# A retention layer and a Mish feed-forward layer: the second product of eight blocks as seven quarter products

## The chip, the cores and the metric

The kernel runs on one core of one Trainium2 chip. Its engines run side by side, each through its own queue in order: TensorE (PE, with its weight loads shown apart as PEld), VectorE (DVE), ScalarE (ACT), GpSimd (POOL) and SyncE (SP), which here issues most of the transfers. The metric is the device time of one launch in microseconds (us).

## What is computed

First a retention layer, a recurrence over 768 steps for 4 batches and 8 heads of width 64; its output, 3072 tokens by 512, goes through two matrix products with Mish between them.

```python
for t in range(S):
    state = gamma[None, :, None, None] * state + np.einsum('bhd,bhe->bhde', k[:, :, t], v[:, :, t])
    y[:, :, t] = scale * np.einsum('bhd,bhde->bhe', q[:, :, t], state)
...
h = x @ w_in                                         # 3072x512 by 512x2048
sp = np.where(h > 20.0, h, np.log1p(np.exp(np.minimum(h, 20.0))))
g = h * np.tanh(sp)
return (g @ w_out).astype(np.float32)                # 3072x2048 by 2048x512
```

## The kernel before

**Chunks and blocks.** The sequence is cut into 24 chunks of 128 tokens, 6 for each batch. The feed-forward part works on 11 blocks: block 0 has 4 chunks, blocks 1 to 10 have two each (256 tokens). Blocks are counted from 0 throughout. Inputs, weights and intermediate values are in fp16 where PE reads them; sums are in fp32 in PSUM.

**A block's two products.** `g1` (line 395) makes one group of the first product, 8 matmuls of 256 columns into one PSUM bank (`h_ps`), and one ACT activation (Mish) from it into a `g` tile that holds two of the 16 slices of 128 rows of the hidden width. Eight groups make the block's first product. The second product takes each of the block's two chunks by itself: 16 matmuls of 512 columns (`g2_mm`, line 410) with a slice of `g` as the stationary operand and a slice of `w_out` as the moving one, summed in one bank (`o_ps`), which DVE copies to SBUF (`g2_out`, line 416). SP stores it. The last chunk of the last block is made in two halves of 256 columns.

**The retention steps** for the next block are put between these matmuls by hand. `casts` (line 209) scales q, k and v into fp16 on POOL. `turn_by_dma` (225) turns q and k by a transfer. `scores_two` (362) makes q times k on PE, and DVE multiplies them by a mask. `outer_two` (369) makes the state's increments on PE; `state` (289) adds and scales them on DVE with L293, or with L296 and L297. `y_two` (379) makes the layer's output from scores and state, and ACT copies it to `xt`, which the next block's first product reads. `next_chunk(g)` (518) casts ahead, turns chunk g and loads chunk g + 2.

**What sets the order.** The kernel is written in the order in which each engine's queue then runs; nothing is rescheduled. The main loop goes through 16 steps u for each block, 8 for the first product and 8 for the second. `plan_of` (524) lists what follows which step: for blocks after the first, casts and `next_chunk` after steps 1, 4, 8 and 12, scores after 7, outer after 10 and y after 13. Stores wait in a list until their step. Tiles come from pools in rotation: the tag `mm` has four PSUM banks for `h_ps` and `o_ps`, the tag `at` two pairs of banks for scores, increments and y. A tile's writer waits until the one that had the buffer before has been read. POOL runs as far ahead as loads and buffers allow, whatever step its casts are written in.

Of the kernel before, what the change touches and what calls it, by code (L numbers as in the profile page):

```python
# [16 lines left out]
def kernel(  # L17
# [150 lines left out]
    def store_due(now):  # L168
        while stores and stores[0][0] <= now:
            _, dst, osb = stores.pop(0)  # L170
            nc.sync.dma_start(dst, osb)
# [223 lines left out]
    def g1(blk, u):  # L395
        nt = BLOCKS[blk] * C
        per = TB // nt
        h_ps = mmps.tile([P, per, nt], FP32, name="h_ps", tag="mm")
        for j in range(per):
            s, f = divmod(u * per + j, FPS)  # L400
            for bp in range(NBP):
                nc.tensor.matmul(  # L402
                    h_ps[:, j], wins[s][f // 2][:, bp, f % 2 * P:(f % 2 + 1) * P], xts[blk][:, bp, :nt],
                    start=(bp == 0), stop=(bp == NBP - 1))
# [1 line left out]
        nc.scalar.activation(gt, h_ps, AF.Mish, scale=inv_boost3)  # L406
# [9 lines left out]
    def g2_out(o_ps, blk, t, due, cols=slice(None)):  # L416
        osb = op.tile(list(o_ps.shape), FP32, name="osb", tag="osb")
        nc.vector.tensor_copy(osb, o_ps)  # L418
# [102 lines left out]

    def plan_of(blk):
        a = first[blk] + 4
        early = blk == 1
        plan = {1: [(cast_to, a + 1)],
                (1 if early else 4): [(cast_to, a + 1), (next_chunk, a)],
                (5 if early else 8): [(cast_to, a + 2)],
                (5 if early else 12): [(cast_to, a + 2), (next_chunk, a + 1)]}  # L530
        if blk + 1 < len(BLOCKS):
            plan[10 if early else 7] = [(scores_two, blk + 1)]
            plan[12 if early else 10] = [(outer_two, blk + 1)]
            plan[14 if early else 13] = [(y_two, blk + 1)]
        return plan

    first_block()
    for blk in range(1, len(BLOCKS)):
# [4 lines left out]
        for u in range(nu):
            store_due(u)
            if u < n1:
                g1(blk, u)
            else:
                t, part = divmod(u - n1, 4)
                if last and t == BLOCKS[blk] - 1:
                    if part % 2 == 0:  # L550
                        half = slice(part // 2 * (d_model // 2), (part // 2 + 1) * (d_model // 2))
                        o_ps = mmps.tile([P, d_model // 2], FP32, name="o_ps", tag="mm")
                        for fb in range(NFB):
                            g2_mm(o_ps, blk, t, fb, half)
                        g2_out(o_ps, blk, t, 0, half)
                        store_due(nu)
                    continue
# [39 lines left out]
```

## Time and profile before

| | |
|---|---|
| median of 3 runs | 214.64 us (214.62 to 214.94) |
| profiled execution, its own time | 214.51 us |
| span of its trace | 212.7 us |
| granted PE clock | 1.000 |
| first matmul of blocks 2, 3, 4, 5 | 67.58, 83.69, 99.59, 115.48 us |
| first matmul of blocks 6, 7, 8, 9, 10 | 131.60, 147.49, 163.39, 179.51, 195.41 us |
| POOL's last cast | 162.79 us |

The profiled execution is 1.8 us longer than the span from its first to its last instruction. Rows of a group give the line, engine, operation, the tile that is written and those that are read, shapes, a count, busy time and the mean of one in ns, and then the idle time ahead of it with what ended it. Rows of a timeline start with the start in us and the length; rows of the same kind are merged, with their count. "Busy" of pipelined matmuls counts overlaps, so a matmul's cost is read from the starts of what stands before and behind it.

### The profile page before, as it was taken

How to read it: one execution, taken by the hardware profiler on the slowest of the kernel's cores; microseconds unless marked ns; L12 is line 12 of the kernel's file. 1: busy time of each engine (PE TensorE's matmuls, PEld its weight loads, DVE VectorE, ACT ScalarE, POOL GpSimd, SP SyncE). 2: the span in 40 equal slices, each digit the busy share in tenths (PEclk: the TensorE clock that was granted, in tenths of full speed). 3: DMA queues.
4: the chain of work that ended last, by engine and by line, in shares of the span. 5: the costliest groups of instructions: out<-in, count | busy, mean ns of one | idle time of the engine just before them, and what ended most of it. 6: DMA issues, size and time to landing. Idle time of an engine off the chain costs nothing.

```text
span 212.7 us, 4169 instructions
## 1 busy us (share of the span) xinstructions
PE 206.9 (97%) x1733; PEld 133.5 (63%) x1733; DVE 84.6 (40%) x113; ACT 77.9 (37%) x122; POOL 75.2 (35%) x72
## 2 busy tenths in 40 slices
PE   7999999999999999999999999999999999999993
PEld 2564444456856856856856856856856856856863
DVE  3697444366046065062064065062065065062011
ACT  2443663153612612612612612612612612612610
POOL 2131000509773662666576067066067000000000
PEclk9999999999999999999999999999999999999999
DMA  5999999998999999999993994994893901101102
GB/s 188 230 231 351 385 386 318 264 256 175 194 235 274 184 241 187 251 217 182 248 220 89 215 182 99 208 178 110 203 196 97 151 0 52 49 2 52 49 0 99
DMA packets 99842, 38.56 MB, mean 181 GB/s; under 512 B 90480, under 2 KB 93808, under 8 KB 99824
## 3 DMA queue, kind: packets, MB, share of 16 engines
q1 hardware_dynamic: 96560, 37.50, 78.7%
q10 hardware_dynamic: 3264, 0.81, 2.3%
q8 instruction: 13, 0.21, 0.4%
q14 instruction: 5, 0.04, 0.1%
HBM read 27.29 MB, written 6.29 MB: 158 GB/s over the span
## 4 chain that ended last, share of the span: by engine, by line
PE 81%; DMA 8%; SPq 6%; ACT 1%; DVE 1%; issue 0%; ACTq 0%
PE h_ps L402 36%; PE o_ps L412 36%; DMA wi<-in_moe_w_in_dram 5%; SPq L120 5%; DMA kf<-in_k_dram 3%; PE y_ps L313 3%; PE at L263 3%; PE y_ps L303 2%; PE u_ps L281 2%; SPq L138 1%; ACT xt L390 1%; SPq L179 0%; DVE win L155 0%; ACT qk L218 0%; PE t_ps L251 0%
## 5 line engine op out<-in xcount | busy, mean ns | idle before, releaser
L412 PE MATMUL o_ps<-wout,g 128*128 128x512 f16 (+1 forms) x400 | 89.2, 371 | 0.0
L402 PE MATMUL h_ps<-xt,win 128*128 128x256 f16 (+1 forms) x704 | 85.7, 282 | 0.6 <-ACT xt L390 0.2
L402 PEld LDWEIGHTS <-win 128*128 128x128 f16 x704 | 68.7, 98 | 18.3 <-DVE win L155 1.1
L406 ACT ACTIVATE g<-h_ps 128x512 f16<-128x512 f32 x96 | 57.3, 597 | 41.2 <-PE h_ps L402 40.6
L412 PEld LDWEIGHTS <-g 128*128 128x128 f16 x400 | 36.9, 98 | 38.0 <-issue 0.3
L273 DVE TENSOR_TENSOR am<-at,tri 128x1024 f16<-128x1024 f32 x20 | 23.6, 1219 | 63.7 <-PE at L263 63.7
L215 POOL TENSOR_TENSOR qk<-qf,qvs 128x512 f16<-128x512 f32 x20 | 20.9, 1045 | 66.2 <-DMA qf<-in_q_dram 58.6
L390 ACT CAST xt<-y_ps 128x1024 f16<-128x1024 f32 x10 | 10.1, 1012 | 62.9 <-PE y_ps L313 62.9
L221 POOL TENSOR_TENSOR v<-vf,qvs 128x512 f16<-128x512 f32 x24 | 25.0, 1042 | 18.0 <-DMA vf<-in_v_dram 16.7
L418 DVE COPY osb<-o_ps 128x512 f32<-128x512 f32 (+1 forms) x25 | 16.5, 666 | 33.4 <-PE o_ps L412 33.4
L220 POOL TENSOR_SCALAR qk<-kf 128x512 f16<-128x512 f32 x18 | 27.8, 1542 | 3.8 <-DMA kf<-in_k_dram 2.5
L241 PE MATMUL at<-ident 128*128 128x512 f16 (+1 forms) x34 | 10.9, 449 | 1.3 <-POOL ident L81 1.3
L296 DVE TENSOR_TENSOR su<-u_ps,st 128x512 f32<-128x512 f32 x13 | 9.0, 692 | 6.4 <-PE u_ps L281 6.2
L297 DVE TENSOR_TENSOR st<-su,gcm 128x512 f16<-128x512 f32 x13 | 10.6, 818 | 0.4
L313 PE MATMUL y_ps<-am,v 128*64 128x128 f16 x192 | 8.2, 223 | 0.2 <-DVE am L273 0.2
L218 ACT ACTIVATE qk<-kf 128x512 f16<-128x512 f32 x6 | 3.8, 630 | 12.1 <-DMA kf<-in_k_dram 12.1
L155 DVE CAST win<-wi 128x1024 f16<-128x1024 f32 x8 | 5.4, 692 | 5.6 <-DMA wi<-in_moe_w_in_dram 5.6
L281 PEld LDWEIGHTS <-qk 128*128 128x128 f16 x80 | 5.3, 98 | 2.7
L303 PEld LDWEIGHTS <-st 128*128 128x128 f16 x80 | 5.3, 98 | 2.7
L313 PEld LDWEIGHTS <-v 128*64 128x64 f16 x192 | 5.8, 109 | 1.7 <-issue 0.3
L281 PE MATMUL u_ps<-v,qk 128*128 128x128 f16 x80 | 6.8, 220 | 0.0
L241 PEld LDWEIGHTS <-ident 128*128 128x128 f16 x34 | 3.5, 114 | 5.1 <-issue 3.3
(42 smaller groups left out, 59.1 us busy)
## 6 DMA issues: line engine op xcount, KB each, us to landing
kf<-in_k_dram SPq DMA_DIRECT2D x23, 256.0 KB, 4.9
vf<-in_v_dram SPq DMA_DIRECT2D x23, 256.0 KB, 5.1
out_dram<-osb SPq DMA_DIRECT2D x23, 256.0 KB, 2.5
qf<-in_q_dram SPq DMA_DIRECT2D x19, 256.0 KB, 4.1
wt<-in_moe_w_out_dram SPq DMA_DIRECT2D x3, 1024.0 KB, 10.1
wi<-in_moe_w_in_dram SPq DMA_DIRECT2D x4, 512.0 KB, 7.3
wi<-in_moe_w_in_dram SPq DMA_DIRECT2D x2, 1024.0 KB, 11.6
qfirst<-in_q_dram SPq DMA_DIRECT2D x2, 512.0 KB, 4.6
```

Source lines behind the costliest of these rows:

```text
L215: nc.gpsimd.tensor_tensor(q16, qf, qs.unsqueeze(2).broadcast_to((P, H, D)), op=ALU.mult)
L220: nc.gpsimd.tensor_scalar(k16, kf, BOOST, None, op0=ALU.mult)
L221: nc.gpsimd.tensor_tensor(v16, vf, vs.unsqueeze(2).broadcast_to((P, H, D)), op=ALU.mult)
L241: nc.tensor.matmul(ats[g][:, 0, :m], ident, ident.unsqueeze(1).broadcast_to((P, m, P)), start=True, stop=True)
L273: nc.vector.tensor_tensor(am[:, :, i:i + n], at[:, :, i:i + n], keep.unsqueeze(1).unsqueeze(1).broadcast_to((P, 2, n, C)), op=ALU.mult)
L281: nc.tensor.matmul(u_ps[:, i], k16[:, 2 * i:2 * i + 2], v16[:, 2 * i:2 * i + 2], start=onto is None or i == 0, stop=onto is None, skip_gro ...
L313: nc.tensor.matmul(y(i)[o:o + 64], v16[:, 2 * i + hh], am[:, hh, i], start=fresh(i), stop=True, skip_group_check=True)
L390: nc.scalar.copy(xt[:, :, :2 * C], y_ps.rearrange("p i j c -> p i (j c)"))
L402: nc.tensor.matmul(h_ps[:, j], wins[s][f // 2][:, bp, f % 2 * P:(f % 2 + 1) * P], xts[blk][:, bp, :nt], start=(bp == 0), stop=(bp == NBP - 1))
L406: nc.scalar.activation(gt, h_ps, AF.Mish, scale=inv_boost3)
L412: nc.tensor.matmul(o_ps, gts[blk, fb][:, t * P:(t + 1) * P], wouts[s][:, f, cols], start=(fb == 0), stop=(fb == NFB - 1))
L418: nc.vector.tensor_copy(osb, o_ps)
```

## The change

From block 3 on, the second product of a block is one product of a 256 x 2048 matrix A (the two chunks of `g`) with the 2048 x 512 matrix B (`w_out`), each cut into quarters. Seven products of quarters (each 8 matmuls of 256 columns) and their sums take the place of the eight that the plain form needs:

- sums of A: S1 = A21 + A22, S2 = S1 - A11, S3 = A11 - A21, S4 = A12 - S2
- sums of B, made once in block 2: T1 = B12 - B11, T2 = B22 - T1, T3 = B22 - B12, T4 = B21 - T2
- C11 = A11 B11 + A12 B21; U2 = A11 B11 + S2 T2; U3 = U2 + S3 T3; C22 = U3 + S1 T1; C12 = U2 + S1 T1 + S4 B22; C21 = U3 + A22 T4

DVE makes the sums in fp16: in each of these blocks 16 operations of 128 x 256 elements, of which the 8 for S1 and S2 (`sums_a`) stand behind groups 4 to 7 of the first product. PSUM sums are kept across products; ACT copies (`snap`) an intermediate value out where it is used twice. DVE adds or copies the four quarters of C into the block's two store tiles. The sums of B take the weights' staging buffers, eight DVE operations of 128 x 1024, one after each of block 2's steps 0 to 7.

The retention steps are moved for these blocks: outer stands after step 0, scores after step 3, y inside the second product between the products S2 T2 and S1 T1. `next_chunk` stands after steps 1 and 7; the stores of a block stand in steps 1 and 2 of the next. Block 2 has `next_chunk` after steps 2 and 8. The last block stores its four quarters one by one.

```diff
+    def weight_sums(half):
+        n, hf = NFB // 2, d_model // 2
...
+        return [
+            lambda: nc.vector.tensor_tensor(t1, b12, b11, op=sub),
+            lambda: nc.vector.tensor_tensor(t2, b22, t1, op=sub),
+            lambda: nc.vector.tensor_tensor(t3, b22, b12, op=sub),
+            lambda: nc.vector.tensor_tensor(t4, b21, t2, op=sub),
+        ]
...
+    def sums_a(blk, u):
+        (s1, s2, _, _), a11, _, a21, a22 = sum_views(blk, u)
+        nc.vector.tensor_tensor(s1, a21, a22, op=ALU.add)
+        nc.vector.tensor_tensor(s2, s1, a11, op=ALU.subtract)
+
+    def sums_b(blk):
+        for u in range(NFB // 4):
+            (_, _, s3, _), a11, _, a21, _ = sum_views(blk, u)
+            nc.vector.tensor_tensor(s3, a11, a21, op=ALU.subtract)
+
+    def sums_c(blk):
+        for u in range(NFB // 4):
+            (_, s2, _, s4), _, a12, _, _ = sum_views(blk, u)
+            nc.vector.tensor_tensor(s4, a12, s2, op=ALU.subtract)
+
+    def seven(blk, hooks, last):
+        n, hf = NFB // 2, d_model // 2
+        ps = [mmps.tile([P, hf], FP32, name="o_ps", tag="mm") for _ in range(3)]
+        pb, pe, px = ps
...
+        def snap(o_ps):
+            x = op.tile([P, hf], FP32, name="snap", tag="snap", bufs=3)
+            nc.scalar.copy(x, o_ps)
+            return x
+
+        def done(i, j, o_ps, plus=None):
+            dst = osb[i][:, j * hf:(j + 1) * hf]
+            if plus is None:
+                nc.vector.tensor_copy(dst, o_ps)
+            else:
+                nc.vector.tensor_tensor(dst, o_ps, plus, op=ALU.add)
...
+        mm(px, a(0, 0), b(0, 0), True)
+        m1 = snap(px)
+        mm(pb, a(0, 1), b(1, 0), True)
+        sums_b(blk)
+        done(0, 0, pb, m1)
+        mm(px, s(2), t(2))
+        u2 = snap(px)
+        sums_c(blk)
+        for fn, *args in hooks:
+            fn(*args)
+        mm(pe, s(1), t(1), True)
+        m5 = snap(pe)
+        mm(px, s(3), t(3))
+        done(1, 1, px, m5)
+        mm(pe, s(4), b(1, 1))
+        done(0, 1, pe, u2)
+        mm(px, a(1, 1), t(4))
+        done(1, 0, px)
+        if not last:
+            for i in range(2):
+                row0 = (first[blk] + i) * P
+                stores.append((1 + i, out[row0:row0 + P], osb[i]))
...
     def plan_of(blk):
         a = first[blk] + 4
-        early = blk == 1
+        if blk >= SEVEN:
+            plan = {1: [(cast_to, a + 1), (next_chunk, a)],
+                    7: [(cast_to, a + 2), (next_chunk, a + 1)]}
+            if blk + 1 < len(BLOCKS):
+                plan[0] = [(outer_two, blk + 1)]
+                plan[3] = [(scores_two, blk + 1)]
+            return plan
...
+        extra = weight_sums(0) + weight_sums(1) if blk + 1 == SEVEN else []
+        for u in range(n1 if blk >= SEVEN else 2 * n1):
             store_due(u)
             if u < n1:
                 g1(blk, u)
+                if blk >= SEVEN and u >= n1 // 2:
+                    sums_a(blk, u - n1 // 2)
...
+            if extra:
+                extra.pop(0)()
+        if blk >= SEVEN:
+            seven(blk, [] if last else [(y_two, blk + 1)], last)
+    store_due(2 * NFB)
```

How DVE's queue changes. Before, these rows are one block's work on DVE, in the order of the queue: the two copies of the second product, the two masks, and the state of two chunks.

```order
L418 COPY osb<-o_ps 128x512 x2
L273 TENSOR_TENSOR am<-at,tri 128x1024 x2
L296 TENSOR_TENSOR su<-u_ps,st 128x512
L297 TENSOR_TENSOR st<-su,gcm 128x512
L296 TENSOR_TENSOR su<-u_ps,st 128x512
```

In the changed kernel, at the end of a block's first product and in its second: the last pair of S1 and S2, S3's four parts, the add that ends C11, S4's four parts, and the add that ends C22. `g_1466` to `g_1529` are the tiles of groups 0 to 3, `g_1562` to `g_1601` those of groups 4 to 7.

```order
L463 TENSOR_TENSOR gsum<-g_1529,g_1601 128x256 [waits Activation_49]
L464 TENSOR_TENSOR gsum<-gsum,g_1529 128x256 [waits DVE_49]
L469 TENSOR_TENSOR gsum<-g_1466 128x256
L469 TENSOR_TENSOR gsum<-g_1493 128x256
L469 TENSOR_TENSOR gsum<-g_1518 128x256
L469 TENSOR_TENSOR gsum<-g_1529 128x256
L510 TENSOR_TENSOR osb<-o_ps,snap 128x256 [waits DMAHW3_49,PE_49,Activation_49]
L474 TENSOR_TENSOR gsum<-g_1562,gsum 128x256
L474 TENSOR_TENSOR gsum<-g_1575,gsum 128x256
L474 TENSOR_TENSOR gsum<-g_1588,gsum 128x256
L474 TENSOR_TENSOR gsum<-g_1601,gsum 128x256 [waits DVE_49]
L510 TENSOR_TENSOR osb<-o_ps,snap 128x256 [waits DMAHW0_49,PE_49,Activation_49]
```

The sums and adds stand in one queue, so the adds for C wait behind all sums that are written ahead of them.

On PE, where the product A12 B21 ends and S2 T2 begins:

```order
L496 MATMUL o_ps<-wout_595,g_1601 128x256
L496 LDWEIGHTS gsum [waits DVE_49]
L496 MATMUL o_ps<-tmat,gsum 128x256 [waits Activation_49]
L496 LDWEIGHTS gsum
L496 MATMUL o_ps<-tmat,gsum 128x256
L496 LDWEIGHTS gsum [waits DVE_49]
```

Every second weight load of this product waits for a part of S2 from DVE, and its first matmul for ACT's copy of the bank that it adds to. Before, the second product waited for activations alone.

On SP, the transfers of one block and the start of the next, before:

```order
L171 DMA out_dram<-osb 128x512 x2
L227 DMA_TRANSPOSE qkt<-qk_1633 128x8x128
L120 DMA qf<-in_q_dram 128x8x64
L120 DMA kf<-in_k_dram 128x8x64
L120 DMA vf<-in_v_dram 128x8x64
L227 DMA_TRANSPOSE qkt<-qk_1740 128x8x128
```

and in the changed kernel:

```order
L173 DMA out_dram<-osb 128x512
L229 DMA_TRANSPOSE qkt<-qk_1760 128x8x128
L122 DMA qf<-in_q_dram 128x8x64
L122 DMA kf<-in_k_dram 128x8x64
L122 DMA vf<-in_v_dram 128x8x64
L173 DMA out_dram<-osb 128x512
L229 DMA_TRANSPOSE qkt<-qk_1870 128x8x128
```

The two stores, which stood together ahead of a pair of chunks, now stand one ahead of each chunk; the first holds the transposes and loads of its block until the block ahead has its C11 and C12.

More of the change, by code (lines that the diff above doesn't have):

```diff
@@ L106 @@
     xts, gts, wins, wouts, wtmps = {}, {}, {}, {}, {}
+    gtiles, tmats, gsums = {}, [], []
+    SEVEN = 3
     nload, ncast = [0], [0]
@@ L424, in g2_out @@
         stores.append((due, dst, osb))
+    def weight_sums(half):
+        n, hf = NFB // 2, d_model // 2
+        if half == 0:
+            tmats.extend(
+                wstage.tile([P, 2, n, hf], FP16, name="tmat", tag="wt", bufs=4)
+                for _ in range(2))
+            gsums.extend(
+                wstage.tile([P, 4, n, P], FP16, name="gsum", tag="wt", bufs=4)
+                for _ in range(2))
+        f = slice(half * FPS, (half + 1) * FPS)
+        t1, t2 = tmats[0][:, 0, f], tmats[0][:, 1, f]
+        t3, t4 = tmats[1][:, 0, f], tmats[1][:, 1, f]
+        b11, b12 = wouts[half][:, :, :hf], wouts[half][:, :, hf:]
+        b21, b22 = wouts[half + 2][:, :, :hf], wouts[half + 2][:, :, hf:]
+        sub = ALU.subtract
+        return [
[4 more added lines that the diff above has]
+        ]
@@ new lines, in sum_views @@
+    def sum_views(blk, u):
+        s = gsums[blk % 2]
+        f = slice(2 * u, 2 * u + 2)
+        lo, hi = gtiles[blk, u], gtiles[blk, u + NFB // 4]
+        return ([s[:, i, f] for i in range(4)],
+                lo[:, :, :P], hi[:, :, :P], lo[:, :, P:], hi[:, :, P:])
+    def sums_a(blk, u):
[6 more added lines that the diff above has]
+            nc.vector.tensor_tensor(s3, a11, a21, op=ALU.subtract)
@@ new lines, in sums_c, with a, b, s @@
+    def sums_c(blk):
[6 more added lines that the diff above has]
+        pb, pe, px = ps
+        osb = [op.tile([P, d_model], FP32, name="osb", tag="osb") for _ in range(2)]
+        def a(i, j):
+            return lambda f: gts[blk, j * n + f][:, i * P:(i + 1) * P]
+        def b(i, j):
+            return lambda f: wouts[(i * n + f) // FPS][:, f % FPS, j * hf:(j + 1) * hf]
+        def s(i):
+            return lambda f: gsums[blk % 2][:, i - 1, f]
+        def t(i):
+            return lambda f: tmats[(i - 1) // 2][:, (i - 1) % 2, f]
+        def mm(o_ps, x, w, first=False):
+            for f in range(n):
+                nc.tensor.matmul(
+                    o_ps, x(f), w(f), start=first and f == 0, stop=f == n - 1,
+                    skip_group_check=True)
+        def snap(o_ps):
[9 more added lines that the diff above has]
+            row0 = (first[blk] + i) * P
+            if last:
+                nc.sync.dma_start(out[row0:row0 + P, j * hf:(j + 1) * hf], dst)
+        mm(px, a(0, 0), b(0, 0), True)
[18 more added lines that the diff above has]
+            for i in range(2):
+                row0 = (first[blk] + i) * P
+                stores.append((1 + i, out[row0:row0 + P], osb[i]))
@@ L525, in plan_of @@
         a = first[blk] + 4
-        early = blk == 1
-        plan = {1: [(cast_to, a + 1)],
[L528 to L534, printed above, removed]
+        if blk >= SEVEN:
[5 more added lines that the diff above has]
+            return plan
+        early, then_seven = blk == 1, blk + 1 == SEVEN
+        plan = {1: [(cast_to, a + 1)],
+                (1 if early else 2 if then_seven else 4): [(cast_to, a + 1), (next_chunk, a)],
+                (5 if early else 8): [(cast_to, a + 2), (next_chunk, a + 1)]}
+        plan[10 if early else 7] = [(scores_two, blk + 1)]
+        plan[12 if early else 10] = [(outer_two, blk + 1)]
+        plan[14 if early else 13] = [(y_two, blk + 1)]
         return plan
@@ L546 @@
                 g1(blk, u)
+                if blk >= SEVEN and u >= n1 // 2:
+                    sums_a(blk, u - n1 // 2)
             else:
                 t, part = divmod(u - n1, 4)
[L549 to L557, printed above, removed]
                 if part == 0:
```

4 lines of the change are left out of this document (1 added, 3 removed).

## The prediction

> **What bounds the kernel now.** I read the page's busy times first, then its chain of waits, then the table of stretches (one row for each block), then the PE timeline inside one block, and last the timelines of the engines that a block's second product would newly wait for.
>
> ```profile
> span 212.7 us, 4169 instructions
> ...
> PE 206.9 (97%) x1733; PEld 133.5 (63%) x1733; DVE 84.6 (40%) x113; ACT 77.9 (37%) x122; POOL 75.2 (35%) x72
> ...
> PE 81%; DMA 8%; SPq 6%; ACT 1%; DVE 1%; issue 0%; ACTq 0%
> PE h_ps L402 36%; PE o_ps L412 36%; DMA wi<-in_moe_w_in_dram 5%; SPq L120 5%; DMA kf<-in_k_dram 3%; PE y_ps L313 3%; PE at L263 3%; PE y_ps L303 2%; PE u_ps L281 2%; SPq L138 1%; ACT xt L390 1%; SPq L179 0%; DVE win L155 0%; ACT qk L218 0%; PE t_ps L251 0%
> ```
>
> PE sets the time: the chain is 81% PE, in equal parts on the two products. DVE and POOL are idle more than half of the span, but that is a mean over stages. The stretches from one block's first L402 to the next's show the stage that counts:
>
> ```profile
> 99.59:115.48 15.89, 15.89 (x141) 10.92 (x140) 6.14 (x7) 5.79 (x9) 10.04 (x9) 1.00 0.96 207
> 147.49:163.39 15.90, 15.90 (x141) 10.90 (x140) 6.56 (x7) 5.79 (x9) 7.35 (x7) 1.00 0.75 162
> 163.39:179.51 16.12, 16.12 (x145) 11.12 (x144) 6.41 (x8) 5.79 (x9) 0.45 (x1) 1.00 0.38 70
> ```
>
> These are blocks 4, 7 and 8 (counted from 0); the columns are length, then busy time of PE, PEld, DVE, ACT, POOL, then clock and DMA. PE is busy all through at full clock. Up to block 7, POOL works 7 to 10 us of each 16; from block 8 on it has nothing left to cast. Inside block 5:
>
> ```profile
> 115.48 7.15 PE L402 MATMUL h_ps<-xt,win 128*128 128x256 f16 x64
> 122.57 0.62 PE L263 MATMUL at<-qkt 64*128 64x128 f16 x16
> 123.12 2.77 PE L412 MATMUL o_ps<-wout,g 128*128 128x512 f16 x12
> 125.72 0.61 PE L281 MATMUL u_ps<-v,qk 128*128 128x128 f16 x8
> 126.17 2.75 PE L412 MATMUL o_ps<-wout,g 128*128 128x512 f16 x12
> 128.76 0.61 PE L303 MATMUL y_ps<-qkt,st 128*128 128x128 f16 x8
> ...
> 129.87 1.90 PE L412 MATMUL o_ps<-wout,g 128*128 128x512 f16 x8
> 131.60 7.15 PE L402 MATMUL h_ps<-xt,win 128*128 128x256 f16 x64
> ```
>
> From start to start, a 512-column matmul costs 2.60 / 12 = 0.217 us. Scores cost 0.55, outer 0.45, y 1.11.
>
> **The change, part by part.**
>
> *Matmuls.* The rates need the length of one:
>
> ```profile
> L412 PE MATMUL o_ps<-wout,g 128*128 128x512 f16 x368 | 85.7, 380 | 0.0
> L402 PE MATMUL h_ps<-xt,win 128*128 128x256 f16 x640 | 71.5, 273 | 0.3 <-ACT xt L390 0.2
> ...
> L418 DVE COPY osb<-o_ps 128x512 f32<-128x512 f32 x23 | 15.6, 686 | 31.1 <-PE o_ps L412 31.1
> ...
> L206 DVE COPY kt<-t_ps 128x512 f16<-128x512 f16 x4 | 1.7, 422 | 0.5 <-PE t_ps L204 0.3
> ...
> L418 DVE COPY osb<-o_ps 128x256 f32<-128x256 f32 x2 | 0.8, 424 | 2.4 <-PE o_ps L412 2.4
> ```
>
> At 256 columns the step is (7.15 - 0.273) / 63 = 0.109 us. Thirty-two at 0.217 (6.93) become 56 at 0.109 (6.12): 0.81 less a block. The first product keeps its 64, and the moved scores, outer and y keep their counts.
>
> *The sums, if nothing disturbs them.* I count from a block's first matmul and put a group of the first product at 8 x 0.109 = 0.87. PE then has outer 0.87 to 1.32, scores 4.05 to 4.60 (0.10 is lost ahead of scores now too: 115.48 + 6.99 is 122.47, they start at 122.57), the last group done at 8.09; then the products A11 8.15, A12 9.02, S2 9.90, y 10.77, S1 11.88, S3 12.76, S4 13.63, A22 14.50 to 15.38. The 0.06 at 8.09 is new: the first product's bank is read by the activation of group 6, which in these rows of block 6 ends 0.597 after 137.98, when PE (from 131.60) is just done:
>
> ```profile
> 132.74 0.60 ACT L406 ACTIVATE g<-h_ps 128x512 f16<-128x512 f32 x1 [1.69 <-PE h_ps L402]
> ...
> 137.98 0.60 ACT L406 ACTIVATE g<-h_ps 128x512 f16<-128x512 f32 x1 [0.28 <-PE h_ps L402]
> ```
>
> An activation ends 0.87 after its group, so the pairs for the sums are there at 6.33, 7.21, 8.08 and 8.96. No row shows a two-input 16-bit DVE operation of 256 elements. From above it is bounded by 0.424 (256 in 32 bits). From below: 512 take 0.422 in 16 bits and 0.686 in 32 bits, so half the streaming goes, and 256 take about 0.29. I take 0.29, since 16 bits are what L206 has. The masks end near 6.84; S2 would be ready between 7.5 and 9.65, its product needs its parts from 9.90 to 10.55; S3 by 10.9 for 12.76, S4 by 12.3 for 13.63. The three ACT copies (0.4 each) and the adds leave 0.1 to 0.2 us. So undisturbed nothing is late, and a block costs 15.4 in place of 16.12: 0.7 less. This holds for blocks 8 and 9 (1.4) and, without y, for 10 (0.75): **2.15 less**.
>
> *The sums beside POOL.* This decides. Here a DVE operation with both inputs in SBUF (L297) meets POOL's casts:
>
> ```profile
> 94.36 1.04 POOL L215 TENSOR_TENSOR qk<-qf,qvs 128x512 f16<-128x512 f32 x1 [1.77 <-DMA qf<-in_q_dram]
> 95.48 1.81 POOL L220 TENSOR_SCALAR qk<-kf 128x512 f16<-128x512 f32 x1
> ...
> 154.83 1.04 POOL L215 TENSOR_TENSOR qk<-qf,qvs 128x512 f16<-128x512 f32 x1 [7.02 <-DMA qf<-in_q_dram]
> ...
> 159.78 1.04 POOL L215 TENSOR_TENSOR qk<-qf,qvs 128x512 f16<-128x512 f32 x1 [1.21 <-DMA qf<-in_q_dram]
> ```
>
> ```profile
> L297 DVE TENSOR_TENSOR st<-su,gcm x13: 691/693/1528, 45.6 to 190.9; 128x512 f16<-128x512 f32 x13
> ...
> 95.08 0.87 DVE L297 TENSOR_TENSOR st<-su,gcm 128x512 f16<-128x512 f32 x1
> 95.87 0.68 DVE L418 COPY osb<-o_ps 128x512 f32<-128x512 f32 x1
> ...
> 155.02 2.35 DVE L273 TENSOR_TENSOR am<-at,tri 128x1024 f16<-128x1024 f32 x2 [6.63 <-PE at L263]
> ...
> 159.84 1.53 DVE L297 TENSOR_TENSOR st<-su,gcm 128x512 f16<-128x512 f32 x1
> ```
>
> Its 13 runs take 0.691 at least and 0.693 in the middle; two of the long ones are shown. Both times it ends 0.55 after POOL's cast does (95.40 to 95.95, 160.82 to 161.37), as if it had waited for the whole cast; and POOL's next cast of k, 1.49 in a row below, stretches to 1.81. The masks, with one input in PSUM, run through POOL's 154.83 cast at full speed. All 16 sums of a block have both inputs in SBUF. The Trainium skill states this as a rule (SBUF — State Buffer, "Who interferes with whom"): such a DVE instruction contends with a GpSimd one that reads SBUF, and whichever has the port blocks the other for its whole length. These rows agree; by the rule 16-bit sums are blocked alike, without it the sum would be the first rival's.
>
> When does POOL work? It casts as loads land, and SP issues them behind the transposes and stores:
>
> ```profile
> 87.23 1.28 SPq L171 DMA_DIRECT2D out_dram<-osb  x2
> ...
> 116.86 1.29 SPq L227 DMA_TRANSPOSE qkt<-qk  x1
> 118.21 0.57 SPq L120 DMA_DIRECT2D qf<-in_q_dram  x1
> ...
> 119.51 0.74 SPq L120 DMA_DIRECT2D vf<-in_v_dram  x1
> ...
> 122.84 0.58 SPq L120 DMA_DIRECT2D qf<-in_q_dram  x1
> ```
>
> ```profile
> 122.00 1.04 POOL L215 TENSOR_TENSOR qk<-qf,qvs 128x512 f16<-128x512 f32 x1 [5.83 <-DMA qf<-in_q_dram]
> 123.16 1.49 POOL L220 TENSOR_SCALAR qk<-kf 128x512 f16<-128x512 f32 x1
> ...
> 125.29 1.04 POOL L221 TENSOR_TENSOR v<-vf,qvs 128x512 f16<-128x512 f32 x1 [0.64 <-DMA vf<-in_v_dram]
> 127.59 1.10 POOL L215 TENSOR_TENSOR qk<-qf,qvs 128x512 f16<-128x512 f32 x1 [1.25 <-DMA qf<-in_q_dram]
> ```
>
> A q load is cast 3.8 to 4.8 after its issue, a v load 5.8. In the new order SP stands each time before the first store of the block ahead, which waits for its last sums of C; that frees it at about -0.3. Store 0.65, transpose 1.3, so q goes out at 1.75, v at 3.05; the second q goes out 4.63 behind the first (122.84 - 118.21), or 0.65 later for the store now between them: 6.4 to 7.0. POOL thus casts q 5.9 to 6.95, k to 8.55, v 8.85 to 9.9, and the second chunk's q, at the middle of 10.2 to 11.8, near 10.9 to 11.95, k to 13.5, v 14.0 to 15.05. That covers the sums almost exactly. A blocked sum of 0.29 ends about 0.15 after the cast; the next cast starts 0.08 after the one ahead and has the port again before the dependent sum behind it. So one sum passes per cast: S2's four parts end at 8.7, 10.05, 10.6, 11.13, S2's product ends 0.65 late (11.43), and y and S1 follow to 13.4. S3's parts come at 12.1, 13.65 and 14.07 (its product ends at 14.4), C11's add at 14.4, S4 behind the second v cast from 15.2 to 15.8, its product at 16.2, and A22, behind the add for C22, ends at 17.2. With v half a microsecond sooner or later, that is 17.7. I take 17.4, 1.45 over the old mean of 63.80 / 4 = 15.95, for blocks 4 to 7: **5.8 more**. The ends: 16.0 if the second chunk lands late and two sums slip in per gap, 18.9 if every cast costs a sum its full length.
>
> *Block 3.* SP still runs behind there (its first store is of block 2), so only one chunk falls on the sums: 0.4 more. *Block 2* gets eight sums of 1024 elements (0.7 each by the same halving) beside six casts; seven precede the masks, whose state and y follow some 2 us later: 0.2 more, at most 0.7. *Stores* of the last block, now four halves, end in the same 256-column copy as before: nothing. SP passes the stores sooner than now; transposes have over 10 us until scores: nothing.
>
> **Sum:** -2.15 + 5.8 + 0.4 + 0.2 = +4.25 on the profiled execution's 214.51 (its span 212.7 and 1.8 around it; the runs' median is 214.64, 0.1% above): 218.8 us.
>
> **Rivals.**
> - *The port does not bite* (POOL's casts fall beside the masks, or 16-bit sums pass). Seven blocks at -0.7 and the last at -0.75: 208.9. For it speaks that casts some 4 us sooner would lie beside the masks; against it, the two collisions above and SP's order, which holds the loads back. It decides if PE waits under 0.7 us a block for the sums.
> - *Sums slip between casts:* an operation that waits for nothing starts before the one ahead ends (the copy at 95.87, L297 ending 95.95), and S3's and S4's parts have no wait among them, so DVE may win the port; that S1 and S2 wait for each other speaks against it. Blocks 4 to 7 at 16.1: -2.15 + 0.6 + 0 to 0.4, about 213.2.
> - *Every cast takes its whole length, or a sum takes 0.424:* 18.5 to 18.9 in blocks 4 to 7, 1 in block 3, 0.7 in block 2: about 225.
> - *Seven products cost PE as much as eight:* against it stands the 0.109 of L402's own 256-column rows; it would add 6.5 to any case. I give it nothing of its own.
>
> **How the numbers follow.** Forecast 0.61 (its own range 215.5 to 222.5); port without effect 0.15; sums slipping 0.13; whole lengths 0.11. The range 209.5 to 224 leaves out most of the first rival's lower half and of the last one's upper. A measurement here tells about 0.2%, 0.4 us: faster 0.25 (first rival, most of the second), same 0.05, slower 0.70.
>
> **What would show it.** In the changed profile: o_ps matmuls of 256 columns at 0.109 where they run freely; gsum operations on DVE of 0.29 alone and 1 us or more beside L215 to L223 casts; PE idle in blocks 4 to 7 ended by DVE, first at S2's third part, then at S3 and S4; blocks 8 and 9 near 15.4. If blocks 4 to 7 are also near 15.4, or gsum operations stay at 0.29 while POOL casts, the forecast is wrong.

## The result and the profile after

The changed kernel takes **208.77 us** (median of 4 runs, 208.5 to 209.76) beside 214.79 us of the kernel before on the same chip (4 runs, 214.62 to 214.98): ratio 0.9728, 95% interval 0.9693 to 0.9763. The forecast was 218.8 us with a range from 209.5 to 224.0; the time came out at the first rival's 208.9, which that range leaves out. The profiled execution took 208.99 us, its span is 207.2 us, its clock was 1.00. Two executions of kernels further down, 259.56 us at a granted clock of 0.757 and 343.38 us at 0.564, are in a second, slower state and stand in no number below (the 211.4 in one expectation still counts the second).

The page of the changed kernel, span, busy times and the chain of waits:

```profile
span 207.2 us, 4659 instructions
...
PE 201.2 (97%) x1909; PEld 150.7 (73%) x1909; DVE 132.2 (64%) x264; ACT 86.6 (42%) x146; POOL 76.2 (37%) x72
...
PE 77%; DMA 8%; SPq 7%; DVE 4%; ACT 1%; issue 1%; ACTq 0%
PE h_ps L404 36%; PE o_ps L496 22%; PE o_ps L415 9%; DMA wi<-in_moe_w_in_dram 5%; SPq L122 5%; DMA kf<-in_k_dram 3%; PE y_ps L315 3%; PE at L265 3%; PE y_ps L305 2%; PE u_ps L283 2%; SPq L140 1%; DVE am L275 1%; DVE gsum L463 1%; ACT xt L392 1%; DVE gsum L464 1%
```

DVE works 132.2 us where it worked 84.6, yet it makes up only 4% of the chain, and PE is still busy 97% of a span that is 5.5 us shorter. The stretches of blocks 4, 5, 7 and 8, each from its first L404 to the next block's (columns as before: length, busy time of PE, PEld, DVE, ACT, POOL, clock, DMA share, GB/s):

```profile
99.21:114.32 15.11, 15.11 (x167) 13.26 (x165) 11.64 (x25) 6.87 (x12) 9.26 (x8) 1.00 1.20 217
114.32:129.92 15.60, 15.50 (x171) 13.40 (x169) 13.18 (x26) 6.87 (x12) 8.99 (x8) 1.00 1.01 170
...
145.26:160.36 15.10, 15.10 (x167) 13.22 (x164) 10.75 (x25) 6.87 (x12) 7.58 (x7) 1.00 0.92 175
160.36:175.69 15.33, 15.33 (x171) 13.50 (x169) 10.50 (x26) 6.87 (x12) 0.50 (x1) 1.00 0.42 71
```

Block 4, with eight operations on POOL, is no longer than block 8 with the end of one (block 8 is 0.22 us longer and has four small matmuls of the retention more, x171 beside x167). So the sums beside POOL's casts, which the forecast priced at 5.8 us, cost next to nothing here. The lengths of all blocks, in us, each the difference of two starts in the PE timeline of the kernel named:

| kernel | block 2 starts | 2 | 3 | 4 | 5 | 6 | 7 | 8 | 9 | 10 to the end |
|---|---|---|---|---|---|---|---|---|---|---|
| before | 67.58 | 16.11 | 15.90 | 15.89 | 16.12 | 15.90 | 15.90 | 16.12 | 15.89 | 17.29 |
| after | 67.99 | 16.12 | 15.10 | 15.11 | 15.60 | 15.34 | 15.10 | 15.33 | 15.10 | 16.41 |

Blocks 4 to 7 were 63.81 and are 61.15. The parts of the difference: blocks 8 to 10 -2.46, blocks 4 to 7 -2.66, block 3 -0.80, block 2 0.01, the start of block 2 +0.41; together -5.50 of 212.7.

A little is lost in blocks 5 and 6. Block 6 takes 0.24 us more than block 7: its last product starts 0.23 late, and the profile names nothing that held it. Block 5 takes 0.27 us more than block 8, which has as many matmuls. Its casts on POOL:

```profile
120.68 1.04 POOL L217 TENSOR_TENSOR qk<-qf,qvs 128x512 f16<-128x512 f32 x1 [4.66 <-DMA qf<-in_q_dram]
121.83 1.49 POOL L222 TENSOR_SCALAR qk<-kf 128x512 f16<-128x512 f32 x1
123.40 1.15 POOL L223 TENSOR_TENSOR v<-vf,qvs 128x512 f16<-128x512 f32 x1
125.86 1.04 POOL L217 TENSOR_TENSOR qk<-qf,qvs 128x512 f16<-128x512 f32 x1 [1.32 <-PE y_ps L305]
126.99 1.61 POOL L222 TENSOR_SCALAR qk<-kf 128x512 f16<-128x512 f32 x1
```

and its sums on DVE, S1 (L463) and S2 (L464) in four pairs, S3 (L469), S4 (L474):

```profile
121.06 0.80 DVE L463 TENSOR_TENSOR gsum<-g,g 128x256 f16<-128x256 f16 x1
121.90 0.68 DVE L464 TENSOR_TENSOR gsum<-gsum,g 128x256 f16<-128x256 f16 x1
122.51 0.28 DVE L463 TENSOR_TENSOR gsum<-g,g 128x256 f16<-128x256 f16 x1
122.82 0.29 DVE L464 TENSOR_TENSOR gsum<-gsum,g 128x256 f16<-128x256 f16 x1
123.03 0.29 DVE L463 TENSOR_TENSOR gsum<-g,g 128x256 f16<-128x256 f16 x1
123.35 0.29 DVE L464 TENSOR_TENSOR gsum<-gsum,g 128x256 f16<-128x256 f16 x1
123.56 1.13 DVE L463 TENSOR_TENSOR gsum<-g,g 128x256 f16<-128x256 f16 x1
124.73 0.29 DVE L464 TENSOR_TENSOR gsum<-gsum,g 128x256 f16<-128x256 f16 x1
124.93 0.89 DVE L469 TENSOR_TENSOR gsum<-g 128x256 f16<-128x256 f16 x4
...
126.07 2.00 DVE L474 TENSOR_TENSOR gsum<-g,gsum 128x256 f16<-128x256 f16 x4
```

The port bites as forecast beside q and v: the L463 at 121.06 ends at 121.86, 0.14 behind the q cast (121.72); the one at 123.56 ends 0.14 behind the v cast (124.55). Beside k's cast it does not: that runs from 121.83 to 123.32, the L464 caught by it ends at 122.58, 0.75 behind its start, and the next three sums start while the cast is still running and take 0.28 or 0.29 each. S3's four parts then pass in the gap between v and the second chunk's q, which begins at +11.54 behind the block's first matmul where the forecast had +10.9. The last S2 part comes late, at 125.02: PE's weight load for it waits 0.38 us, and that is the loss.

```profile
125.07 0.11 PEld L496 LDWEIGHTS <-gsum 128*128 128x128 f16 x2 [0.38 <-DVE gsum L464]
```

### The profile page after: what moved, and what is told of

Read it like the earlier page. It is cut to its first block, busy times and chain, and to the rows that moved or that the text cites. A ratio compares the mean times of both kernels' runs of the same rounds, so it can differ in the third digit from the quotient of the medians.

```text
span 207.2 us, 4659 instructions
## 1 busy us (share of the span) xinstructions
PE 201.2 (97%) x1909; PEld 150.7 (73%) x1909; DVE 132.2 (64%) x264; ACT 86.6 (42%) x146; POOL 76.2 (37%) x72
## 4 chain that ended last, share of the span: by engine, by line
PE 77%; DMA 8%; SPq 7%; DVE 4%; ACT 1%; issue 1%; ACTq 0%
PE h_ps L404 36%; PE o_ps L496 22%; PE o_ps L415 9%; DMA wi<-in_moe_w_in_dram 5%; SPq L122 5%; DMA kf<-in_k_dram 3%; PE y_ps L315 3%; PE at L265 3%; PE y_ps L305 2%; PE u_ps L283 2%; SPq L140 1%; DVE am L275 1%; DVE gsum L463 1%; ACT xt L392 1%; DVE gsum L464 1%
## 5 line engine op out<-in xcount | busy, mean ns | idle before, releaser
L404 PE MATMUL h_ps<-xt,win 128*128 128x256 f16 (+1 forms) x704 | 88.0, 282 | 0.8 <-DVE win L157 0.4
L404 PEld LDWEIGHTS <-win 128*128 128x128 f16 x704 | 67.8, 98 | 17.3 <-DVE win L157 1.3
L415 PE MATMUL o_ps<-wout,g 128*128 128x512 f16 x128 | 30.1, 380 | 0.0
L496 PEld LDWEIGHTS <-gsum 128*128 128x128 f16 x256 | 24.3, 98 | 3.9 <-DVE gsum L464 0.4
L496 PE MATMUL o_ps<-tmat,gsum 128*128 128x256 f16 x192 | 23.7, 273 | 0.1
L415 PEld LDWEIGHTS <-g 128*128 128x128 f16 x128 | 11.7, 98 | 13.0 <-issue 0.3
L496 PEld LDWEIGHTS <-g 128*128 128x128 f16 x192 | 18.8, 98 | 2.4 <-issue 0.2
L510 DVE TENSOR_TENSOR osb<-o_ps,snap 128x256 f32<-128x256 f32 x24 | 10.2, 423 | 14.3 <-ACT snap L502 11.2
L463 DVE TENSOR_TENSOR gsum<-g,g 128x256 f16<-128x256 f16 x32 | 13.8, 430 | 6.3 <-ACT g L408 6.2
L496 PE MATMUL o_ps<-wout,g 128*128 128x256 f16 x128 | 15.3, 273 | 0.0
L502 ACT COPY snap<-o_ps 128x256 f32<-128x256 f32 x24 | 8.9, 373 | 13.9 <-PE o_ps L496 8.4
L464 DVE TENSOR_TENSOR gsum<-gsum,g 128x256 f16<-128x256 f16 x32 | 11.1, 347 | 1.1
L474 DVE TENSOR_TENSOR gsum<-g,gsum 128x256 f16<-128x256 f16 x32 | 9.9, 370 | 0.0
```

The source lines that it names most:

```text
L404: nc.tensor.matmul(h_ps[:, j], wins[s][f // 2][:, bp, f % 2 * P:(f % 2 + 1) * P], xts[blk][:, bp, :nt], start=(bp == 0), stop=(bp == NBP - 1))
L415: nc.tensor.matmul(o_ps, gts[blk, fb][:, t * P:(t + 1) * P], wouts[s][:, f, cols], start=(fb == 0), stop=(fb == NFB - 1))
L463: nc.vector.tensor_tensor(s1, a21, a22, op=ALU.add)
L464: nc.vector.tensor_tensor(s2, s1, a11, op=ALU.subtract)
L496: nc.tensor.matmul(o_ps, x(f), w(f), start=first and f == 0, stop=f == n - 1, skip_group_check=True)
```

## The experiments

Each theory had to say why POOL's casts cost so little. The runs first measure the port by itself, then take the change apart, then put back, one by one, what the prediction had assumed.

**The port alone.** A kernel without the layers sends one cast on POOL and one 256-element sum on DVE, the sum after a delay of 0.2 to 1.2 us, for both kinds of cast; then rows of four casts beside twelve sums. It leaves out the whole computation.

> Not the layer: only casts on POOL (128x512, 32 to 16 bits) and sums on DVE (128x256, 16 bits), started together and with the sum put back by 0.2 to 1.2 us. Theory A (the port is held for a time that the operation sets): a sum that meets the two-input cast (TENSOR_TENSOR, 1.04) ends 0.15 after the cast does; a sum that meets the one-input cast (TENSOR_SCALAR, 1.49) ends about 0.75 after that cast began, and one that starts later than 0.6 into it takes its 0.29. In the rows of twelve sums beside four casts, twelve that wait for nothing run 0.21 apart once the first has the port, and the cast waits; twelve that wait for each other let casts in between them. Theory B (as predicted): every cast holds the port for its whole length and only one sum passes per cast in both rows of twelve, so they take as long as four casts. Sums with one input in PSUM run free under both.

POOL's rows, the two-input cast (L56) and the one-input cast (L60):

```profile
3.77 1.04 POOL L56 TENSOR_TENSOR cast<-raw,scale_t 128x512 f16<-128x512 f32 x1 [3.35 <-ACT raw L53]
...
19.51 1.49 POOL L60 TENSOR_SCALAR cast<-raw 128x512 f16<-128x512 f32 x1 [2.26 <-ACT raw L53]
...
24.87 1.49 POOL L60 TENSOR_SCALAR cast<-raw 128x512 f16<-128x512 f32 x1 [1.19 <-ACT raw L53]
...
33.95 4.19 POOL L56 TENSOR_TENSOR cast<-raw,scale_t 128x512 f16<-128x512 f32 x4 [1.81 <-ACT raw L53]
...
50.74 6.30 POOL L60 TENSOR_SCALAR cast<-raw 128x512 f16<-128x512 f32 x4 [4.71 <-ACT raw L53]
```

and DVE's sums beside them:

```profile
3.81 1.15 DVE L66 TENSOR_TENSOR sum<-ga,gb 128x256 f16<-128x256 f16 x1
...
19.55 0.72 DVE L66 TENSOR_TENSOR sum<-ga,gb 128x256 f16<-128x256 f16 x1
...
25.43 0.28 DVE L66 TENSOR_TENSOR sum<-ga,gb 128x256 f16<-128x256 f16 x1
...
34.00 5.91 DVE L66 TENSOR_TENSOR sum<-ga,gb 128x256 f16<-128x256 f16 x12
...
50.78 3.35 DVE L66 TENSOR_TENSOR sum<-ga,gb 128x256 f16<-128x256 f16 x12
...
64.81 2.51 DVE L66 TENSOR_TENSOR sum<-ga,gb 128x256 f16<-128x256 f16 x12
```

Beside the two-input cast the sum ends at 4.96, 0.15 behind the cast's end (4.81). Beside the one-input cast it ends at 20.27, 0.76 behind the cast's start; less the same 0.15, the port was held for about 0.60 of 1.49 us. A sum that starts 0.56 after the cast (25.43 against 24.87) takes its 0.28. Twelve sums beside four two-input casts take 5.91 us, one passing for each cast and the rest behind them; beside four one-input casts 3.35; alone 2.51. So Theory A holds for the time that each kind of cast holds the port, but not for the row beside two-input casts: it had the sums run on and the casts wait, and one sum passed per cast, as Theory B had it. Twelve sums with one input in PSUM take 0.42 each beside four casts, none of them longer than the others.

The Trainium skill (SBUF — State Buffer, "SBUF: two separate sides") has the port held for the whole instruction: the two-input casts agree (0.15 behind their end), k's one-input cast does not (0.60 of 1.49 us), and the measurement decides.

**Eight quarter products** in the changed order, without any sums: the retention steps alone.

```diff
-        mm(px, s(2), t(2))
...
+        pair(px, 0, 0)
+        pair(pb, 0, 1, hooks)
+        pair(pe, 1, 0)
+        pair(mmps.tile([P, hf], FP32, name="o_ps", tag="mm"), 1, 1)
...
-                if blk >= SEVEN and u >= n1 // 2:
-                    sums_a(blk, u - n1 // 2)
```

> The retention steps stand as in the changed kernel, but the second product is made of eight quarter products without any sums (64 matmuls of 256 columns). If the gain is the eighth product alone: 8 x 0.87 = 7.0 us slower than the changed kernel, about 215.7. If moving the retention steps brought part of it, less: 212 to 214.

215.43 us (214.93 to 216.45), ratio 1.0029, interval 1.0006 to 1.0051. Blocks 3 and 4 take 15.98 each. The moved steps bring no gain by themselves (with the second product in 64 matmuls of half the width, they cost 0.3%); the 6.7 us between this kernel and the changed one are the eighth product, 8 x 0.109 = 0.87 a block for eight blocks (7.0), less what the sums cost.

**The sums of A left out.** The products read slices of g in their place.

```diff
-            return lambda f: gsums[blk % 2][:, i - 1, f]
+            return a(1, 0) if i < 4 else a(0, 1)
...
-        sums_b(blk)
...
-        sums_c(blk)
...
-                if blk >= SEVEN and u >= n1 // 2:
-                    sums_a(blk, u - n1 // 2)
```

> Leaves out the 16 sums of A on DVE in each block (its products read quarters of g in their place). Theory A: PE's waits in blocks 5 and 6 go (15.60 and 15.34 become 15.33 and 15.10), all else stays: 0.5 us less, 208.2. Rival: the sums also cost elsewhere (the port slows POOL's casts and so loads, ACT's copies come late): 1 us or more less.

208.48 us (208.18 to 208.71), ratio 0.9698, interval 0.9651 to 0.9746. All the sums of A, with every cast that they meet, cost some 0.3 us of 208.77, less than the intervals can tell. Blocks 5 and 6 take 15.33 and 15.11 there, as expected.

**The changed kernel again**, for a second trace beside later runs.

> The changed kernel itself, on the chip of the kernels beside it: 208.5 to 209 us, blocks 3 to 9 at 15.1 or 15.33 but for waits of 0.2 to 0.5 us in one to three of the blocks 4 to 7.

208.69 us (208.34 to 209.01), ratio 0.9724, interval 0.9709 to 0.9738. Block 5 takes 15.33 here: its 0.3 us over block 8 is not there in each execution. Block 6 takes 15.32, near the first trace's 15.34.

**k's cast with two inputs**, which is shorter (1.04 in place of 1.49 us) but holds the port throughout.

```diff
+    boost = cpool.tile([P, H], FP32, name="boost")
...
+    nc.vector.memset(boost, BOOST)
...
-            nc.gpsimd.tensor_scalar(k16, kf, BOOST, None, op0=ALU.mult)
+            nc.gpsimd.tensor_tensor(
+                k16, kf, boost.unsqueeze(2).broadcast_to((P, H, D)), op=ALU.mult)
```

> POOL casts k with two inputs (1.04 us) in place of one (1.49). Theory A: a sum that meets k's cast now waits for up to 1.04 and not 0.6, S2's parts in blocks 5 to 7 come 0.2 to 0.4 later: 0.5 to 1.2 us slower, 209.3 to 210. Theory B (a cast holds the port for its whole length, and the casts merely fell well): k's casts are 0.45 shorter, so waits shrink: 208.3 to 208.8.

210.22 us (209.71 to 211.12), ratio 0.978, interval 0.9731 to 0.9829; blocks 4 to 7 take 15.33, 15.93, 15.82 and 15.13. A cast that is 0.45 us shorter makes the kernel some 1.5 us slower; the intervals of the two ratios overlap a little, but the trace shows 1.06 us of it in blocks 4 to 7. The loss is not where I had expected it: PE waits for a part of S4, 0.24 us in block 5 and 0.49 in block 6, more than for S2. What counts is how long the port is held, not how long POOL is busy.

**v cast twice**, so that the gap behind v is gone.

```diff
-        nc.gpsimd.tensor_tensor(
-            v16, vf, vs.unsqueeze(2).broadcast_to((P, H, D)), op=ALU.mult)
+        for _ in range(2 if g >= CPB + 8 else 1):
+            nc.gpsimd.tensor_tensor(
+                v16, vf, vs.unsqueeze(2).broadcast_to((P, H, D)), op=ALU.mult)
```

> From chunk 12 on POOL casts v a second time into the same tile, so two two-input casts follow one another in each chunk. Refined theory (such a cast lets one sum through, the one-input cast of k holds the port for 0.6): S2's last part comes about 0.75 later in blocks 4 to 7, and S4's parts meet the second chunk: 0.7 to 1.5 us more in each of four blocks, 211.5 to 215 in all. If placement were all that matters and DVE had slack of more than a cast: under 209.5.

211.9 us (210.08 to 212.26), ratio 0.9856, interval 0.9814 to 0.9899. Block 3, which I had not named, loses most: it takes 16.31 in place of 15.10; PE waits there for a part of S2, as its timeline shows:

```profile
94.84 0.92 PE L497 MATMUL o_ps<-tmat,gsum 128*128 128x256 f16 x4 [0.72 <-DVE gsum L465]
```

Blocks 3 to 7 together take 79.05 in place of 76.25, 2.8 us more.

**A pause between S3's and S4's parts**, a DVE write without inputs (0.11 us), in case a row of sums keeps POOL out.

```diff
+    pad = cpool.tile([P, 64], FP32, name="pad")
...
             nc.vector.tensor_tensor(s3, a11, a21, op=ALU.subtract)
+            nc.vector.memset(pad, 0.0)
...
             nc.vector.tensor_tensor(s4, a12, s2, op=ALU.subtract)
+            nc.vector.memset(pad, 0.0)
```

> A short DVE write without inputs (64 elements) stands behind each part of S3 and S4, so no two of these sums run directly one behind the other. If a row of sums keeps the port and makes POOL wait, breaking it lets casts in: S4 comes later in blocks 4 to 7, 0.3 to 1 us more in each, 210 to 212; blocks 8 to 10, without casts, stay at 15.1 or 15.33. If the rows do not matter: 208.8.

208.61 us (208.27 to 208.99), ratio 0.9721, interval 0.9706 to 0.9735: no difference, against what I had expected if the rows mattered. The same pause beside the two-input cast of k:

> Both together, k cast with two inputs and the rows of sums broken: this gives POOL back what the prediction had taken for granted, casts that hold the port throughout and one sum per cast. Refined theory: more than either alone, 1 to 2 us in each of blocks 4 to 7, 212 to 217 (the prediction said 218.8 for casts of k of 1.49). If the two don't add up: as k alone, 210.2.

210.97 us (3 executions, 210.06 to 211.85), ratio 0.9829, interval 0.9781 to 0.9878, below the 212 to 217 expected. It lies 0.75 us over the kernel without the pause, and the intervals overlap, so that this does not show a cost of its own.

**k's cast holding the port for some 1.7 us**, a little longer than the prediction had it (1.49): the two-input cast, and three of its heads cast again. The hold comes in two pieces, with a gap of 0.08 us between them.

```diff
-            nc.gpsimd.tensor_scalar(k16, kf, BOOST, None, op0=ALU.mult)
+            nc.gpsimd.tensor_tensor(
+                k16, kf, boost.unsqueeze(2).broadcast_to((P, H, D)), op=ALU.mult)
+            nc.gpsimd.tensor_tensor(
+                k16[:, :3], kf[:, :3], boost[:, :3].unsqueeze(2).broadcast_to((P, 3, D)),
+                op=ALU.mult)
```

> POOL casts k with two inputs (1.04) and casts three of the eight heads again (about 0.45), so that k's cast holds the port for about 1.5, as the prediction had it. If the length for which k's cast holds the port is the step that failed, this is where the loss comes back: 1 to 3 us over the k cast of 1.04, 211 to 213.5. If the prediction was right in all else: 216 to 219. If k's hold does not matter: 210.

212.45 us (212.0 to 213.2), ratio 0.9893, interval 0.9857 to 0.9928: 3.7 us come back of the 10 that the forecast was too high. Blocks 3 to 7 take 15.34, 15.37, 16.74, 16.35 and 15.42. Block 4 shows why it is not more. Its casts, from v to the second chunk's q:

```profile
107.96 1.09 POOL L229 TENSOR_TENSOR v<-vf,qvs 128x512 f16<-128x512 f32 x1
110.79 1.05 POOL L219 TENSOR_TENSOR qk<-qf,qvs 128x512 f16<-128x512 f32 x1 [1.74 <-PE y_ps L311]
```

and the sums (S1, S2, S3 are L469, L470, L475 in this kernel):

```profile
108.07 1.13 DVE L469 TENSOR_TENSOR gsum<-g,g 128x256 f16<-128x256 f16 x1
109.23 0.29 DVE L470 TENSOR_TENSOR gsum<-gsum,g 128x256 f16<-128x256 f16 x1
...
109.97 0.89 DVE L475 TENSOR_TENSOR gsum<-g 128x256 f16<-128x256 f16 x4
```

S3's four parts are through at 110.86, just as the second q begins, 11.44 behind the block's first matmul at 99.35. The pause added to this kernel as well:

> The same, with S3's and S4's rows broken by short writes without inputs. The prediction's rule in full (casts hold throughout, one sum per cast): 216 to 219 by the prediction, 211.5 to 215 by what two-input casts of 1.04 with broken rows gave (211.4).

212.19 us (211.73 to 213.04), ratio 0.9873, interval 0.9841 to 0.9905: again no difference, and below the 216 to 219 of the prediction's rule.

**The second chunk sooner.** The second store of a block goes out behind the second chunk's loads, and the casts have a sixth buffer, so that none waits for y; with k's long hold.

```diff
-    castp = ctx.enter_context(tc.tile_pool(name="rn_cast", bufs=5))
+    castp = ctx.enter_context(tc.tile_pool(name="rn_cast", bufs=6))
...
-                stores.append((1 + i, out[row0:row0 + P], osb[i]))
+                stores.append((1 + 2 * i, out[row0:row0 + P], osb[i]))
...
-                    7: [(cast_to, a + 2), (next_chunk, a + 1)]}
+                    2: [(cast_to, a + 2), (next_chunk, a + 1)]}
```

> The k cast holds the port for about 1.7 us, as in the run before, and now the second chunk's loads go out ahead of the block's second store, with a sixth buffer for the casts so that none waits for y. Placement theory (what keeps blocks 4 to 7 cheap with a port held throughout is the gap ahead of the second chunk's q cast, which lies 0.5 us later than the prediction put it and in some blocks waits for y): the second q comes at 10.2 to 10.9 behind a block's first matmul, S3's parts meet casts in all four blocks, these take 16.3 to 17.4 each in place of 15.4 to 16.7, and the time is 214.0 to 218.0 us. Rival (DVE finds its gaps wherever the second chunk lies; the prediction's count of one sum for each cast is wrong by itself): blocks 4 to 7 stay as they are with k's long hold, 211.5 to 213.0 us.

214.58 us (9 executions from 212.81 to 215.1), ratio 0.9964, interval 0.9937 to 0.9992: the whole gain of the change but 0.4% is gone. The same kernel again, with the trace that is read here:

> The same kernel once more, for a trace at full clock: by the placement theory, which its time of 214.6 us bears out, blocks 4 to 7 at 16.0 to 17.0 us, the second q's cast at 10.2 to 10.9 us behind a block's first matmul, and S3's parts each behind a cast; by the rival, 15.4 to 16.7 as with k's long hold alone, and the 2 us come from elsewhere.

214.14 us (212.46 to 215.33), ratio 0.9964, interval 0.9925 to 1.0002. The lengths are 15.50 for block 3, then 15.59, 16.76, 16.30 and 16.37, 65.02 for blocks 4 to 7. Their second q casts begin at +11.23, +10.67, +10.27 and +10.96, where the forecast had +10.9; the first and the last are later than I expected, and block 4's 15.59 lies in the range of the rival alone. PE in block 5, from the last groups of the first product, and where it waits in blocks 6 and 7:

```profile
120.54 3.67 PE L410 MATMUL h_ps<-xt,win 128*128 128x256 f16 x32
124.04 1.91 PE L502 MATMUL o_ps<-wout,g 128*128 128x256 f16 x16
125.79 0.60 PE L502 MATMUL o_ps<-tmat,gsum 128*128 128x256 f16 x4
126.59 0.39 PE L502 MATMUL o_ps<-tmat,gsum 128*128 128x256 f16 x2 [0.20 <-DVE gsum L470]
127.86 0.39 PE L502 MATMUL o_ps<-tmat,gsum 128*128 128x256 f16 x2 [0.89 <-DVE gsum L470]
...
147.21 1.05 PE L502 MATMUL o_ps<-wout,gsum 128*128 128x256 f16 x8 [0.64 <-DVE gsum L480]
...
164.17 0.39 PE L502 MATMUL o_ps<-wout,gsum 128*128 128x256 f16 x2 [0.66 <-DVE gsum L480]
```

and DVE and POOL in block 6, where S3's four parts (the L475 row) meet q's cast and both of k's:

```profile
143.16 2.94 DVE L475 TENSOR_TENSOR gsum<-g 128x256 f16<-128x256 f16 x4
...
146.36 1.40 DVE L480 TENSOR_TENSOR gsum<-g,gsum 128x256 f16<-128x256 f16 x4
```

```profile
142.98 1.17 POOL L219 TENSOR_TENSOR qk<-qf,qvs 128x512 f16<-128x512 f32 x1 [0.74 <-DMA qf<-in_q_dram]
144.19 1.04 POOL L224 TENSOR_TENSOR qk<-kf,boost 128x512 f16<-128x512 f32 x1
145.32 0.64 POOL L226 TENSOR_TENSOR qk<-kf,boost 128x192 f16<-128x192 f32 x1
145.91 1.09 POOL L229 TENSOR_TENSOR v<-vf,qvs 128x512 f16<-128x512 f32 x1
```

With its two assumptions made nearly true, the prediction's mechanism appears. In block 5 PE idles for the third and fourth part of S2 (0.20 + 0.89), and y starts at +12.14, 1.43 later than undisturbed; the forecast had 0.65. In block 6 S3's row takes 2.94 in place of 0.89: in the trace one part ends 0.14 behind q's cast, one 0.14 and one 0.35 behind k's first, and one 0.15 behind k's second. So two parts pass in the gap between k's two casts, which a single long cast does not have. S4 makes PE wait 0.64 in block 6 and 0.66 in block 7.

The same move **with the changed kernel's own k cast**:

> The same move of the second store and the sixth buffer in the changed kernel itself, with its own k cast. Placement theory: S3's parts then meet the second q's cast, but three of them and of S4 pass beside k's cast behind its first 0.6 us, so blocks 4 to 7 lose 0.2 to 0.6 each: 209.2 to 211.2 us. Rival: no difference that can be told, 208.3 to 209.0 us.

208.97 us (208.72 to 209.55), ratio 0.9729, interval 0.9707 to 0.975, blocks 4 to 7 at 15.10, 15.33, 15.33, 15.10. Against my expectation of 209.2 to 211.2, the place of the second chunk by itself does not matter. S3 under the second q takes 1.74 us in place of 0.89 in block 5, but S4 behind it passes beside k's cast in 0.96:

```profile
124.78 1.74 DVE L469 TENSOR_TENSOR gsum<-g 128x256 f16<-128x256 f16 x4
...
126.78 0.96 DVE L474 TENSOR_TENSOR gsum<-g,gsum 128x256 f16<-128x256 f16 x4
```

4.2 us over blocks 4 to 7 (65.02 less 60.86) lie between these two kernels, which differ in k's hold alone. At the changed kernel's own place of the second chunk the long hold had cost 3.0 us there (63.88 in all): k's hold makes most of the loss, and the sooner chunk adds to it only beside a long hold.

**Seven products from block 2 on**, to see whether a ninth block gains too.

```diff
-    SEVEN = 3
+    SEVEN = 2
```

> Seven products from block 2 on, the weights' sums in block 1. One block more: 0.8 less, 208.0, if block 2's sums stay clear of the casts; with waits as in blocks 5 and 6: 208.3; if block 1's weight sums push back block 2's masks and state: 208.8 or more.

209.23 us (208.95 to 209.92), ratio 0.9736, interval 0.9708 to 0.9764: no gain. That is the time of my third case, but by another cause: block 2 takes 16.95 in place of 16.12, since the scores, now four steps sooner, wait for a transpose:

```profile
73.82 0.40 PE L265 MATMUL at<-qkt 64*128 64x128 f16 x8 [1.30 <-DMA qkt<-qk]
```

**Stores behind the loads** (due in steps 6 and 7, the second chunk at step 5), which brings q's casts in blocks 4 to 7 forward by 2 to 6 us.

```diff
-                stores.append((1 + i, out[row0:row0 + P], osb[i]))
+                stores.append((6 + i, out[row0:row0 + P], osb[i]))
...
-                    7: [(cast_to, a + 2), (next_chunk, a + 1)]}
+                    5: [(cast_to, a + 2), (next_chunk, a + 1)]}
```

> Each block's two stores stand behind both transposes and loads of the next block, so SP no longer waits for the last sums of C before it loads: casts come some 3 to 5 us sooner, most of them beside masks and state. The waits of blocks 4 to 6 (0.2 to 0.5 us in all) go or move to other blocks: 208.2 to 208.7. If casts fall on S2 instead: 209 to 210.

208.57 us (208.47 to 209.13), ratio 0.9706, interval 0.9682 to 0.973: not to be told from the changed kernel. No version beats it by more than the intervals leave open.

## Why the prediction was wrong, step by step

- **The matmuls: right.** Forecast 0.81 less a block by 256-column matmuls at 0.109. Undisturbed blocks lose 0.79 or 0.80 (15.89 to 15.10, 16.12 to 15.33), the last one 0.88 where 0.75 was forecast. Blocks 8 to 10 gave 2.46, forecast 2.15: the 0.06 for an activation and the 0.1 to 0.2 for copies and adds did not show.
- **The sum's length: right.** Taken as 0.29 between two bounds, and S3's 32 operations, one group in the trace, lie between 0.279 and 0.289:

```profile
L469 DVE TENSOR_TENSOR gsum<-g x32: 279/285/289, 93.8 to 199.7; 128x256 f16<-128x256 f16 x32
```

- **The port: right for q and v, wrong for k. This is the step that failed.** The text took every cast to hold the port for its whole length, from rows in which the blocking cast was always q's two-input one; k's 1.81 was read as a sign of the same, but it only showed k waiting. "So one sum passes per cast" then left no room for the eight dependent sums. k's cast, the longest of the three, frees the port after 0.60 us: three sums pass beside its rest in block 5. Worked through again with 0.60 for k and all else kept (an estimate), the forecast's own timeline has the last parts of S2, S3 and S4 at 10.4, 12.1 and 13.4, each ahead of the matmul that reads it, and the block at its undisturbed 15.4 in place of 17.4: by this estimate the step alone makes 8 us in blocks 4 to 7. The other way round, the runs bring back only a part. With a k cast that holds 1.7 us, the time rises by 3.7 us, and with the second chunk near where the forecast had it by 5.2 to 5.6 (214.14 and 214.58 against 208.97).
- **The second chunk's place: off by half a microsecond or more**, at +11.45 to +12.98 in blocks 4 to 7 in place of +10.9, in part because its q cast waits for y. That alone costs or saves nothing (208.97), but with k's long hold it is worth the difference from 212.45 to 214.14 or 214.58. (The forecast's terms for q's issue, -0.3, 0.65 and 1.3, add up to 1.65 and not to its 1.75; that changes nothing here.)
- **One timeline for four blocks: the rest.** The forecast had 17.4 for each of blocks 4 to 7 (69.6); with both assumptions made nearly true they take 65.02. In that trace S2 makes PE lose 1.43 us in block 5 and S4 makes it wait some 0.65 in blocks 6 and 7, where S2 costs 0.33 and 0.19 (S2's product takes 1.37 and 1.23 in place of 1.04). No block has both in full, as the forecast had it for all four, and in block 4 no wait of that size shows. The first q is cast at +6.05, +5.63 and +5.34 in blocks 5 to 7; only block 5 has the 5.9 of the forecast, and it comes nearest, with 16.76. How these 4.6 us divide between the landing times, the gap in k's long hold and the rest of the count stays open: no run set the landings to one time, and none held the port for k in one piece.
- **Block 3, forecast 0.4 more,** took 0.80 less, in part by the same error: with k's long hold it takes 15.34 and 15.50 in place of 15.10. **Block 2's weight sums, 0.2 more,** cost nothing: three meet casts (1.37, 1.09 and 1.09 in place of 0.69), but the masks behind them wait for the scores anyway.
- **The first rival** had the time (208.9) by a wrong reason: the port does bite. What decides is what it named as its test, that PE waits for the sums less than 0.7 us a block: at most 0.38 in the rows of block 5. That its time was met is therefore luck in part.
- **The second rival** (213.2, sums slip between casts) saw something that is there: once under way, S4's row makes q's cast wait (1.63 in place of 1.04, below). But breaking up the rows changed nothing that can be told (208.61), so this is not what saved the time.
